# Two passes of the first expert at 208 columns instead of 256

## The chip, the cores and the metric

The kernel runs on one core of a Trainium2 chip. The metric is device time in microseconds of one launch, lower is better. TensorE multiplies, VectorE and ScalarE move and convert, GpSimd (POOL in the profile) issues the transfers with computed addresses, SyncE (SP) most of the others.

## What is computed

A recurrent attention (4 batches, 8 heads, 768 steps, 48 features a head) makes 3072 rows of 384 features; a mixture of 8 experts then works on these rows. Each row goes to the one expert with the largest logit.

```python
for t in range(S):
    cur = np.einsum('bhd,bhe->bhde', u[None] * kt, vt)
    y[:, :, t] = np.einsum('bhd,bhde->bhe', rt, state + cur)
    state = w[None, :, :, None] * state + np.einsum('bhd,bhe->bhde', kt, vt)
...
logits = x @ w_gate
expert_idx = np.argmax(logits, axis=1)
...                                   # rows are numbered within their expert
h = np.maximum(np.einsum('ecd,edf->ecf', disp, w1), 0.0)     # 384 -> 1024
y = np.einsum('ecf,efd->ecd', h, w2)                         # 1024 -> 384
out[i] = gate_w[i] * y[expert_idx[i], pos[i]]
```

With the reference's inputs the first expert gets 380 rows in all, 272 of them from the first 2048 rows; no expert gets more than 410.

## The kernel before, in words

**Attention** works on 24 tiles of 128 steps, one after the other. Behind each tile come its logits and its routing (`route`): the row's number within its expert is counted, and the row is scattered into a buffer in device memory, `xsd`, that has a region for each expert.

**Experts** work in passes. `PASSES` (line 25) has one entry per pass: the expert, the first row, the rows per gathered tile q, the rows of each tile that are handed out qo, and the number of tiles m. A pass fetches m tiles with q rows each from `xsd` (`gather`, line 274), turns them on TensorE to columns (`xtrans`, line 291), so that a pass works on n = m x q columns, and runs two layers. Experts 1 to 7 have one pass of 4 x 104 = 416 columns. The first expert has two: its first rows are taken while the attention still runs (`early_places`, `gather(0)` at tile 20), so that its first pass can start when the attention ends; the second pass does the rest. The first pass gathers tiles of 128 rows of which 80 are handed out, 160 rows in 256 columns; the second has 2 x 128 = 256 rows.

**A product in two parts.** Weights and rows are each split in a high part, in the four-byte type `float32r`, and a rest. A product is three matmuls: high x high, high x rest, rest x high. Layer 1 (`layer1`, lines 308 to 310) makes 8 blocks of 128 outputs from 3 parts of the input, 72 matmuls a pass; layer 2 (`layer2`, lines 327 to 329) makes 3 blocks from 8 parts, 72 as well. Each matmul has its own 128x128 weights. ScalarE makes the high part (`xh` line 295, `hh` line 313), VectorE the rest (`xl` line 296, `hl` line 314), and VectorE copies layer 2's result (`yt`, line 330). `finish` (line 343) turns a tile of the result back and `emit` scales it (line 334) and scatters it to the output (line 335).

**Weights** of the next expert are fetched by SyncE during a pass (line 241) and split by ScalarE and VectorE (lines 249, 250); each `next(ws)` does a piece of it.

**Order.** It is written out by hand: the calls stand in program order, and each engine works in that order. In the last attention tile the first pass's transposes come before the attention's last products; three blocks of its layer 1 are woven into the routing of the last tile. Lines 411 and 92 also matter below: products in full precision (type `float32`), 4 calls of 128 columns, and one of 16 columns a tile.

**When the shortcut fails.** `flags` (line 206) sets a flag if the first 16 tiles (`SNAP`) hold fewer rows of the first expert than `EARLY` while more come later; a branch at the end then does that expert again.

Of the kernel before, what the change touches and what calls it, by code (L numbers as in the profile page):

```python
# [17 lines left out]
NT, DM, E, F = 3072, 384, 8, 1024  # L18
# [2 lines left out]
NI = B * NC  # L21
NP = H // 2
W1S, WL = 416, 416
EARLY, SNAP = 160, 16
PASSES = [(0, 0, 128, EARLY // 2, 2), (0, EARLY, 128, 128, 2)] + [(e, 0, WL // 4, WL // 4, 4) for e in range(1, E)]
XW = 400
FAR = 65536.0
PLAN = [((0, 1, 2), ())] + [((n // 2 + 3,) if n % 2 == 0 and n < 8 else (), (n,)) for n in range(14)]
# [6 lines left out]
def rwkv_moe(nc, tc, dmj, rkv, bdc, wv, wu, uv, wg, w1, w2, out, cap):  # L35
# [4 lines left out]
    with ExitStack() as ctx:  # L40
# [12 lines left out]
        idf = const.tile([128, NI], F32, name="idf")  # L53
        pos = const.tile([128, len(PASSES), 4], F32, name="pos")
        pen = const.tile([128, len(PASSES), 4], F32, name="pen")
        pidx = const.tile([128, len(PASSES), 4], I32, name="pidx")
        cs = const.tile([128, E + 2], F32, name="cs")
# [158 lines left out]
        with ExitStack() as mc:  # L216
# [54 lines left out]
            def gather(k):  # L271
                q, m = PASSES[k][2], PASSES[k][4]
                for i in range(m):
                    nc.gpsimd.indirect_dma_start(out=xg[k % 2][:q, i].bitcast(I32), out_offset=None, in_=xsd[:, :],  # L274
                                                 in_offset=bass.IndirectOffsetOnAxis(ap=pidx[:q, k, i:i + 1], axis=0),
                                                 bounds_check=E * NT - 1, oob_is_err=False)

            def take(k):
                q, m = PASSES[k][2], PASSES[k][4]
                t = keep.tile([128, 4], I32, tag="ids", name=f"ids{k}", bufs=2)  # L280
                g = keep.tile([128, 4], F32, tag="gw", name=f"gw{k}", bufs=2)
                nc.vector.scalar_tensor_tensor(out=t[:q, :m], in0=pen[:q, k, :m], scalar=FAR, in1=xg[k % 2][:q, :m, DM], op0=ALU.mult, op1=ALU.add)
                nc.vector.tensor_copy(out=g[:q, :m], in_=xg[k % 2][:q, :m, DM + 1])
                ids[k] = t, g

            def xtrans(k, j):
                q, m = PASSES[k][2], PASSES[k][4]
                pool, tag, bufs = ((ps1, "a1", 1) if k else (psA, "a0", 2), (ps1, "u", 1), (psA, "a0", 2) if k < 2 else (ps1, "a1", 1))[j]
                tp = pool.tile([128, m * q], F32, tag=tag, name=f"tp{k}_{j}", bufs=bufs)
                for i in range(m):  # L290
                    nc.tensor.transpose(out=tp[:, q * i:q * i + q], in_=xg[k % 2][:q, i, 128 * j:128 * j + 128],  # L291
                                        identity=idn[:q, :q])

                def split():
                    nc.scalar.copy(out=xh[:, j, :m * q], in_=tp)  # L295
                    nc.vector.tensor_tensor(out=xl[:, j, :m * q], in0=tp, in1=xh[:, j, :m * q].bitcast(F32), op=ALU.subtract)  # L296

                return split
# [694 lines left out]
```

## Time and profile before

| | us |
|---|---|
| runs | 396.44, 397.38, 399.80 |
| median | 397.38 |
| the profiled execution | 397.02 |
| its span | 395.3 |

| engine | busy us | share of the span |
|---|---|---|
| TensorE (PE) | 375.1 | 95% |
| weight loads (PEld, beside PE) | 338.4 | 86% |
| VectorE (DVE) | 237.2 | 60% |
| ScalarE (ACT) | 204.4 | 52% |
| GpSimd (POOL) | 137.7 | 35% |

Busy times come from one execution, recorded by the hardware profiler; an engine that waits is not busy. Matmuls overlap, so the distance between the starts of two says more than the duration of one. The attention lies in about the first 136 us, the passes behind it.

### The profile page before, as it was taken

What the parts mean: (1) busy time and instruction counts of PE and PEld (TensorE: products, weight loads), DVE (VectorE), ACT (ScalarE), POOL (GpSimd) and SP (SyncE); (2) the same over time, 40 slices, a digit from 0 to 9 for tenths busy, and PEclk for the clock granted to TensorE, in tenths of its full rate; (3) what the DMA queues carried; (4) which work ended last, traced back from release to release, by engine and by line L of the source; (5) the groups of instructions that cost most, each with busy time, mean ns of one, the idle gap of its engine ahead of it and who ended that gap; (6) DMA issues with size and microseconds to landing.
All of it is one profiled execution on the core that took longest, in us unless ns stands there. A gap on an engine that the chain in (4) does not pass through costs nothing.

```text
span 395.3 us, 9463 instructions
## 1 busy us (share of the span) xinstructions
PE 375.1 (95%) x3587; PEld 338.4 (86%) x3590; DVE 237.2 (60%) x574; ACT 204.4 (52%) x556; POOL 137.7 (35%) x199
## 2 busy tenths in 40 slices
PE   7999999999989789799999999999999999999993
PEld 3677778777767589799999999999999999999992
DVE  6897889898887466554645645645645645643210
ACT  3668787888578334534624624624624624722301
POOL 6122538585673426601501601601601601201203
PEclk9999999999999899999999999999999999999998
DMA  8999878888722546641634644644644644400102
GB/s 174 260 241 263 219 218 236 259 238 264 200 82 71 175 132 189 203 124 21 209 109 131 177 129 133 176 133 133 183 131 127 185 135 129 144 4 16 44 1 70
DMA packets 20633, 59.93 MB, mean 152 GB/s; under 512 B 4303, under 2 KB 4451, under 8 KB 20577
## 3 DMA queue, kind: packets, MB, share of 16 engines
q1 hardware_dynamic: 14848, 44.12, 40.6%
q0 software_dynamic: 5600, 14.72, 11.5%
q8 instruction: 30, 0.49, 0.6%
q10 hardware_dynamic: 128, 0.39, 0.4%
q14 instruction: 27, 0.21, 0.2%
HBM read 49.98 MB, written 10.03 MB: 152 GB/s over the span
## 4 chain that ended last, share of the span: by engine, by line
PE 74%; issue 12%; ACT 5%; DVE 3%; POOL 2%; DMA 1%; POOLq 1%; another core or an unknown queue 0%; SPq 0%; ACTq 0%; DVEq 0%
PE a L310 8%; PE a L309 8%; PE a L308 8%; PE b L327 7%; PE b L328 7%; PE b L329 7%; PE y L565 6%; PE a L522 6%; PE y L556 3%; PE xp L104 3%; PE c L92 2%; ACT s L503 2%; PE c L82 2%; PE tp L291 2%; PE u L534 2%
## 5 line engine op out<-in xcount | busy, mean ns | idle before, releaser
L335 POOL DMA_INDIRECT out<-yo,ids x32 | 32.3, 1009 | 168.1 <-ACT yo L334 166.2
L308 PE MATMUL a<-xh,ws 128*128 128x416 f32 (+1 forms) x216 | 75.3, 349 | 2.2 <-issue 2.0
L313 ACT ACTIVATE hh<-a 128x416 fp32r<-128x416 f32 (+1 forms) x72 | 35.2, 489 | 74.1 <-PE a L310 69.2
L327 PE MATMUL b<-hh,ws 128*128 128x416 f32 (+2 forms) x216 | 73.4, 340 | 0.0
L309 PE MATMUL a<-xl,ws 128*128 128x416 f32 (+1 forms) x216 | 72.5, 336 | 0.1
L310 PE MATMUL a<-xh,ws 128*128 128x416 f32 (+1 forms) x216 | 72.4, 335 | 0.0
L328 PE MATMUL b<-hl,ws 128*128 128x416 f32 (+2 forms) x216 | 71.7, 332 | 0.3 <-issue 0.3
L329 PE MATMUL b<-hh,ws 128*128 128x416 f32 (+2 forms) x216 | 71.5, 331 | 0.0
L314 DVE SCALAR_TENSOR_TENSOR hl<-a,hh 128x416 fp32r<-128x416 f32 (+1 forms) x72 | 39.8, 553 | 50.8 <-ACT hh L313 38.7
L250 DVE TENSOR_TENSOR ws<-wr,ws 128x384 fp32r<-128x384 f32 (+1 forms) x112 | 67.6, 618 | 2.3 <-ACT ws L249 2.3
L503 ACT ACTIVATE s<-eye,l 128x128 f32<-128x128 f32 x168 | 53.8, 392 | 17.2 <-DVE l L93 16.2
L249 ACT CAST ws<-wr 128x384 fp32r<-128x384 f32 (+1 forms) x112 | 60.0, 558 | 2.2 <-DMA xsd<-xr,slot 2.2
L330 DVE COPY yt<-b 128x416 f32<-128x416 f32 (+2 forms) x27 | 14.6, 542 | 66.7 <-PE b L329 64.3
L492 POOL TENSOR_TENSOR P<-dm 112x512 f32<-112x512 f32 x21 | 27.5, 1312 | 48.7 <-DVE dm L508 20.2
L308 PEld LDWEIGHTS a<-xh,ws 128*128 128x128 f32 x216 | 40.7, 188 | 3.3 <-issue 2.4
L328 PEld LDWEIGHTS b<-hl,ws 128*128 128x128 f32 x216 | 40.8, 189 | 0.8 <-issue 0.5
L309 PEld LDWEIGHTS a<-xl,ws 128*128 128x128 f32 x216 | 40.7, 188 | 0.8 <-DVE xl L296 0.5
L329 PEld LDWEIGHTS b<-hh,ws 128*128 128x128 f32 x216 | 40.6, 188 | 0.4
L327 PEld LDWEIGHTS b<-hh,ws 128*128 128x128 f32 x216 | 40.8, 189 | 0.2
L310 PEld LDWEIGHTS a<-xh,ws 128*128 128x128 f32 x216 | 40.6, 188 | 0.4
L274 POOL DMA_INDIRECT xg<-xsd,pidx x32 | 35.0, 1093 | 15.1 <-issue 7.0
L295 ACT CAST xh<-tp 128x416 fp32r<-128x416 f32 (+1 forms) x27 | 12.6, 480 | 52.3 <-PE tp L291 52.3
(147 smaller groups left out, 569.8 us busy)
## 6 DMA issues: line engine op xcount, KB each, us to landing
wr<-w SPq DMA_DIRECT2D x24, 512.0 KB
wr<-w SPq DMA_DIRECT2D x32, 384.0 KB
bd<-bdc SPq DMA_DIRECT2D x24, 384.0 KB
dm<-dmj SPq DMA_DIRECT2D x40, 192.0 KB
dm<-dmj SPq DMA_DIRECT2D x6, 256.0 KB
xg<-xsd,pidx POOLq DMA_INDIRECT x32
out<-yo,ids POOLq DMA_INDIRECT x32
dm<-dmj ACTq DMA_DIRECT2D x2, 192.0 KB
```

The source lines that it names most:

```text
L249: nc.scalar.copy(out=hi, in_=r)
L250: low.append(lambda: nc.vector.tensor_tensor(out=lo, in0=r, in1=hi.bitcast(F32), op=ALU.subtract))
L274: nc.gpsimd.indirect_dma_start(out=xg[k % 2][:q, i].bitcast(I32), out_offset=None, in_=xsd[:, :], in_offset=bass.IndirectOffsetOnAxis(ap=p ...
L308: nc.tensor.matmul(a, lhsT=wh, rhs=xh[:, d, :n], start=d == 0, stop=False)
L309: nc.tensor.matmul(a, lhsT=wh, rhs=xl[:, d, :n], start=False, stop=False)
L310: nc.tensor.matmul(a, lhsT=wl, rhs=xh[:, d, :n], start=False, stop=d == 2)
L313: nc.scalar.activation(hh[:, f, :n], a, AF.Relu)
L314: nc.vector.scalar_tensor_tensor(out=hl[:, f, :n], in0=a, scalar=0.0, in1=hh[:, f, :n].bitcast(F32), op0=ALU.max, op1=ALU.subtract)
L327: nc.tensor.matmul(o, lhsT=wh, rhs=hh[:, f, :n], start=f == 0, stop=False)
L328: nc.tensor.matmul(o, lhsT=wh, rhs=hl[:, f, :n], start=False, stop=False)
L329: nc.tensor.matmul(o, lhsT=wl, rhs=hh[:, f, :n], start=False, stop=f == 7)
L503: nc.scalar.mul(out=s[:, h, p], in_=eye, mul=bon)
```

## The change

`EARLY` goes from 160 to 208. The first pass gathers two tiles of 104 rows and hands out all of them; the second starts at row 208 and has two tiles of 104 rows. Both passes work on 208 columns instead of 256, and together they still cover 416 rows. The condition on the first 16 tiles now asks for 208 rows.

```diff
-EARLY, SNAP = 160, 16
-PASSES = [(0, 0, 128, EARLY // 2, 2), (0, EARLY, 128, 128, 2)] + [(e, 0, WL // 4, WL // 4, 4) for e in range(1, E)]
+EARLY, SNAP = 208, 16
+PASSES = [(0, 0, EARLY // 2, EARLY // 2, 2), (0, EARLY, 104, 104, 2)] + [(e, 0, WL // 4, WL // 4, 4) for e in range(1, E)]
```

On TensorE the two programs have the same 2277 rows in the same order. This is a piece of the difference at the start of the second pass; `tp` is a turned tile, `yp` a turned result, and the sizes are rows by columns of what is written or streamed (the numbers behind names are buffers).

```order
-L291 MATMUL tp_2_2821<-idn,xg_102 128x128 x2
-L343 MATMUL yp_0_2826<-idn,yt 80x128 x3
-L343 MATMUL yp_1_2835<-idn,yt 80x128 x3
-L308 MATMUL a_0_2844<-xh,ws_0_977 128x256
+L291 MATMUL tp_2_2821<-idn,xg_102 128x104 x2
+L343 MATMUL yp_0_2826<-idn,yt 104x128 x3
+L343 MATMUL yp_1_2835<-idn,yt 104x128 x3
+L308 MATMUL a_0_2844<-xh,ws_0_977 128x208
```

No row has changed its place; the turned tile and the matmul of layer 1 have fewer columns, the turned result of the first pass more rows. ScalarE shows the same, here at the end of the attention, where the first pass's tiles are converted (`xh`) between the attention's results (`xs`).

```order
-L295 CAST xh<-tp_0_2418 128x256
-L295 CAST xh<-tp_1_2421 128x256
+L295 CAST xh<-tp_0_2418 128x208
+L295 CAST xh<-tp_1_2421 128x208
 L569 COPY xs_2450<-y_0_2432 128x2x128
 L569 COPY xs_2450<-y_1_2433 128x2x128
```

The two casts stand where they stood, ahead of the copies of the attention's last result, with 48 columns less.

## Rows read from the trace of the kernel before

**Rows 1.** The page's first part: busy us (share of span) xinstructions

```profile
PE 375.1 (95%) x3587; PEld 338.4 (86%) x3590; DVE 237.2 (60%) x574; ACT 204.4 (52%) x556; POOL 137.7 (35%) x199
```

**Rows 2.** Busy us by stage: stretch, length, engines (instructions), PEclk, DMA share, GB/s

```profile
136.00:143.10 7.10, 5.49 (x51) 4.55 (x49) 3.55 (x18) 3.35 (x14) 2.57 (x4) 1.00 0.17 60
143.10:157.70 14.60, 14.29 (x120) 14.05 (x120) 9.68 (x35) 5.49 (x13) 7.75 (x7) 1.00 0.70 205
...
160.00:170.60 10.60, 8.38 (x68) 7.96 (x68) 5.50 (x12) 5.21 (x15) 6.06 (x6) 1.00 0.59 186
170.60:180.30 9.70, 9.70 (x87) 9.70 (x86) 3.92 (x11) 1.99 (x5) 0.00 (x0) 1.00 0.32 97
180.30:383.00 202.70, 202.70 (x1159) 198.56 (x1158) 99.59 (x191) 88.02 (x184) 47.98 (x46) 1.00 0.40 119
```

**Rows 3.** Waits of 128 to 182 us: us in total, times, longest

```profile
PE a L308 <- issue: 2.0, 1, 2.0
...
PEld a L309 <- DVE xl L296: 0.5, 2, 0.3
PE ct L180 <- ACT hh L313: 0.4, 1, 0.4
...
PE b L328 <- issue: 0.3, 1, 0.3
...
PE a L308 <- DVE hl L314: 0.2, 1, 0.2
```

**Rows 4.** Groups by line and shape, whole span: busy us, mean ns, idle before

```profile
L308 PE MATMUL a<-xh,ws 128*128 128x256 f32 x48 | 14.2, 296 | 2.2 <-issue 2.0 <-DVE hl L314 0.2
...
L296 DVE TENSOR_TENSOR xl<-tp,xh 128x416 fp32r<-128x416 f32 x21 | 12.2, 583 | 1.0 <-ACT xh L295 1.0
L291 PE MATMUL tp<-idn,xg 104*128 104x104 f32 x84 | 10.9, 252 | 0.0
L295 ACT CAST xh<-tp 128x416 fp32r<-128x416 f32 x21 | 10.7, 509 | 45.9 <-PE tp L291 45.9
...
L92 PE MATMUL c<-pick,ct 128*128 128x16 f32 x54 | 10.6, 271 | 5.0 <-ACT ct L87 4.3 <-issue 0.4
...
L296 DVE TENSOR_TENSOR xl<-tp,xh 128x256 fp32r<-128x256 f32 x6 | 2.3, 418 | 1.4 <-ACT xh L295 1.4
...
L295 ACT CAST xh<-tp 128x256 fp32r<-128x256 f32 x6 | 2.0, 380 | 6.4 <-PE tp L291 6.4
```

**Rows 5.** Timeline of TensorE: start us, us, line, operation, out<-in, shape, count

```profile
152.03 0.28 PE L327 MATMUL b<-hh,ws 128*128 128x256 f32 x1
...
157.62 0.28 PE L329 MATMUL b<-hh,ws 128*128 128x256 f32 x1
157.74 0.82 PE L291 MATMUL tp<-idn,xg 128*128 128x128 f32 x6
158.39 0.82 PE L343 MATMUL yp<-idn,yt 128*80 128x128 f32 x6
...
159.36 0.39 PE L309 MATMUL a<-xl,ws 128*128 128x256 f32 x1
...
186.17 0.35 PE L309 MATMUL a<-xl,ws 128*128 128x416 f32 x1
...
194.23 0.35 PE L310 MATMUL a<-xh,ws 128*128 128x416 f32 x1
```

**Rows 6.** Timeline of weight loads, 9.9 to 11.2 us

```profile
9.91 0.30 PEld L92 LDWEIGHTS c<-pick,ct 128*128 128x128 f32 x2 [0.65 <-ACT ct L87]
10.13 0.97 PEld L411 LDWEIGHTS gp<-wd,ft 128*128 128x128 f32 x8
11.02 0.21 PEld L458 LDWEIGHTS <-wz 128*128 128x128 bf16 x2
```

**Rows 7.** Timeline of TensorE, transposes of 104 columns

```profile
170.61 0.52 PE L291 MATMUL tp<-idn,xg 104*128 104x104 f32 x4
```

**Rows 8.** Timeline of ScalarE and TensorE around 167 us

```profile
167.03 0.38 ACT L313 ACTIVATE hh<-a 128x256 fp32r<-128x256 f32 x1 [2.76 <-PE a L310]
...
167.93 0.39 PE L308 MATMUL a<-xh,ws 128*128 128x256 f32 x1 [2.04 <-issue]
```

## The prediction

> **What bounds the kernel now.** I read the page first, for the engine that is full; then busy time by stage, to see where the two passes that change lie and whether that engine is still full there; then the waits of that stretch; then the starts of single matmuls and weight loads, because the change alters the size of a matmul and nothing else.
>
> TensorE is busy 95% of the span, no other engine over 60% [rows 1]. By stage [rows 2] the two passes of the first expert run from about 136 to 180.3 us. TensorE is full in 143.1 to 157.7 (14.29 of 14.60 us) and in 170.6 to 180.3 (9.70 of 9.70). It has holes in 136 to 143.1 (5.49 of 7.10), where the routing of the last tile is woven in, and in 160 to 170.6 (8.38 of 10.60). From 180.3 to 383 it is busy all 202.70 us. So what these two passes win or lose on TensorE goes straight to the end: behind them nothing waits that could swallow it. The granted clock is 1.00 in all these stages, the 2.4 GHz level.
>
> The holes in the passes' own work [rows 3] are one wait of 2.0 us before L308, one of 0.3 before L328, and small ones of 0.2 to 0.5 us behind evictions.
>
> **The change, part by part.** No row is moved, added or removed on TensorE: shapes change, and nothing else. Five things get a price.
>
> *The 288 matmuls, 256 columns before, 208 after* (72 in each layer of each pass; [rows 4] has L308's 48, and the other five lines have as many). What counts is not the duration of one (296 ns there, they overlap) but the distance between starts. From 152.03 to 157.62 us stand 48 matmuls of 256 columns: 5.59 / 47 = 0.119 us each. From 186.17 to 194.23 stand 44 of 416: 8.06 / 43 = 0.187 [rows 5]. That is 0.068 us for 160 columns, 0.43 ns a column. Were columns all that counts, 208 would take 0.119 - 48 x 0.00043 = 0.098 us.
>
> But each of these matmuls has a weight load of its own, 128x128 of four-byte data, whatever its columns. How fast such loads can follow one another is seen where the matmul is short: L411's eight loads start at 10.13 and the next line's at 11.02, so they are 0.89 / 8 = 0.111 us apart, with 128 columns per matmul; as the eight are shown to last 0.97 us, one lasts 0.97 - 7 x 0.111 = 0.19, and L92's two, 0.30 us together, start 0.30 - 0.19 = 0.11 us apart, with 16 columns per matmul [rows 4, 6]. From 128 columns down to 16 nothing is won, so this is the load. At 256 columns the interval (0.119) stands just above that floor, at 208 the columns alone (0.098) would lie under it. I take the floor, 0.111: L411's row is the nearest in columns. The saving is 0.119 - 0.111 = 7.6 ns before rounding. I count 261 matmuls: the 27 of the first three blocks of layer 1 lie in the stage from 136 to 143.1, where TensorE waits for others. 261 x 7.6 ns = **2.0 us**. Bounds: 0 (the interval stays), and 261 x 20.6 ns = 5.4 us (columns alone).
>
> The Trainium skill, "TensorE: Matmul & The Clock Gate", section "Back-to-back issue gap", gives columns / 2.4 + 2.5 ns for a lone matmul: an estimate of 89 ns at 208, 20 ns under its 109 at 256, which by itself would give 5.2 us. Its section "LDWEIGHTS (loading the stationary operand)" gives columns of the weights / 1.2, 107 ns for 128, which sets against that a floor close to the 0.11 us of the rows; no run so far shows which of the two binds at 208.
>
> *The 12 transposes* (L291), 128 columns before, 104 after. Six start at 157.74 and the next line at 158.39: 0.108 us each; four of 104 columns take 0.52 us, one of them 0.25: (0.52 - 0.25) / 3 = 0.09 each [rows 4, 5, 7]. Six lie on the full path: **0.1 us**. The other six lie in 131 to 136, ahead of waits: nothing.
>
> *Evictions* with 48 columns less. ScalarE's cast takes 380 ns at 256 and 509 at 416, 0.81 ns a column, 39 ns saved; VectorE's subtraction 418 and 583, 1.03 a column, 49 ns saved [rows 4]. They are hidden behind TensorE except at the small waits (twice for xl, once for hh, once for hl) [rows 3]: about 0.09 each where both stand in the chain, **0.3 us**, or nothing if another releaser is next.
>
> *Outputs.* The first expert's four result tiles have 104 rows where they had 80, 80, 128, 128. ScalarE's multiply there keeps its 384 columns. The gathers fetch 104 rows for 128, the scatters as many tiles as before. All this lies behind full stretches of TensorE: nothing.
>
> *The count the early pass relies on.* The first pass now wants 208 rows of the first expert among the first 16 tiles, where it wanted 160. From the reference's inputs there are 272, and the expert has 380 in all, under 416. The branch that would do the expert again is not taken: nothing.
>
> Sum, against the profiled execution's own 397.02 us (its span of 395.3 and 1.7 around it): 397.02 - 2.0 - 0.1 - 0.3 = **394.6 us**. The median of the three runs is 397.38, 0.4 above that execution; one per cent either side of it is 393.4 and 401.4, about what a measurement of this kernel can tell from no change.
>
> **The rivals.**
> *Columns alone count* (the load hides better than I think). For it: at 256 and 416 the interval follows the columns. Against: L92 and L411 stop at 0.11. It gives 397.02 - 5.4 - 0.4 = 391.2 us. The skill's gap formula above points this way.
>
> *The gain is lost to a wait that TensorE does not set.* At 167.03 ScalarE starts L313, 2.76 us after its last work, although the last matmul of the block it reads, the fourth block of nine, was started by 159.36 + 34 x 0.119 = 163.4; TensorE's L308 follows at 167.93 [rows 5, 8]. The trace names no reason for ScalarE's late start. If its moment is fixed by something else, all that is won before 167.93 is lost, and only the 90 matmuls behind it count: 90 x 7.6 ns = 0.7, 396.2 us with 0.1 for the rest. The 0.3 us before L328 [rows 3] could grow in the same way. Against: if ScalarE is late by its place in its own program, the delay moves along with the work. If the late start goes away altogether, up to 2.0 us are won on top.
>
> *Slower: narrow four-byte matmuls lose their rate.* This is the one that ends on the other side. The matmuls with operands in the rounded four-byte type run at 0.43 ns a column, about one period of 2.4 GHz, and every row of that kind in the trace has 256 columns or more. All four-byte work with fewer goes at about two periods a column or slower: transposes of 128 columns 0.108 us, of 104 columns 0.09 [rows 4, 5, 7], and L411, a product in full precision, takes two instructions of 0.111 us for each of its four calls [rows 6]. Should 208 columns fall under that rule, one costs 208 x 0.85 = 177 ns, and 288 x 58 ns = 16.8 us: 414 us. If each also had to be done twice, like L411, 354 ns and 288 x 235 = 67.7 us: 465 us. The point that decides is whether the fast rate hangs on the number of columns, somewhere between 208 and 256. Against it: the built instruction streams of TensorE have the same length in both kernels, and in those 288 matmuls the column count is all that differs, so no slower form is chosen when the program is made; only the engine itself could do so. No row of the trace contradicts it, so it keeps a chance that is not small.
>
> **How the numbers follow.** Load-bound at about 0.111 us: 0.60, at 394.6, with 393.0 to 396.0 around it (a floor of 0.107 to 0.115). Columns alone: 0.12, at 391.2. Gain lost in a wait: 0.13, at 396 to 398. Narrow matmuls slow: 0.15, at 414 to 465. The likeliest is 394.6. The range that leaves out the slow rival and little else is 391.0 to 398.0; the likeliest one's own is 393.0 to 396.0. Faster by over 1% (under 393.4): the 0.12 and a small part of the first case, 0.17. Slower by over 1%: 0.15, and 0.01 for what I don't see: 0.16. Within 1%: 0.67.
>
> **What would show it right or wrong.** In the profile after, 48 matmuls of layer 2 in the first pass that took 5.59 us should take 47 x 0.111 = 5.2 us; 4.6 us would speak for columns alone, 5.6 for no effect, 8.3 or more for the slow rival. The weight loads should start 0.111 us apart, each right behind the one before. ScalarE's row that is now late by 2.76 us should be about as late, and shifted to the left with the rest. The stretch of pass 2 to the end should last the same, from its first L308 on (now 180.28), and start 2.4 us sooner. The prediction is wrong if the interval is anything but 0.107 to 0.115 us, or if a hole grows by more than a microsecond.

## The result, and the profile after

The changed kernel took 392.78 us in the median of four runs (391.35 to 394.80), the kernel before 397.40 beside it; the ratio is 0.989, 95% interval 0.985 to 0.994. Two later comparisons on other chips, with more runs, gave 0.993 (0.990 to 0.996) and 0.993 (0.989 to 0.997). In microseconds that is 4.3 the first time and 2.8 both other times, where 2.4 were forecast (the medians themselves lie 4.6, 3.4 and 3.7 us apart). 392.78 lies inside the range given (391.0 to 398.0) and just under the likeliest case's own (393.0 to 396.0); against the bound of 1% it came out faster by 1.1% once and within the bound, by 0.7%, twice. The kernel's own time differs between chips: the kernel before took 387.9, 394.9, 395.0 and 397.6 us on four of them. So times are compared on one chip only.

The page of the profile after (span 391.0 us, 395.3 before), its busy times, as in [rows 1]:

```profile
PE 373.2 (95%) x3587; PEld 337.6 (86%) x3590; DVE 236.5 (60%) x574; ACT 203.7 (52%) x556; POOL 138.8 (36%) x199
```

Busy time by stage, columns as in [rows 2] (the last three numbers are the granted clock, the DMA share and GB/s):

```profile
131.00:136.00 5.00, 5.00 (x50) 3.99 (x48) 3.38 (x18) 2.02 (x7) 1.42 (x2) 0.66 0.45 149
136.00:143.10 7.10, 5.51 (x49) 4.94 (x49) 4.34 (x26) 2.66 (x10) 1.76 (x3) 0.92 0.29 87
143.10:157.70 14.60, 14.60 (x125) 14.60 (x123) 9.31 (x32) 5.89 (x16) 8.01 (x7) 0.92 0.66 196
...
160.00:170.60 10.60, 10.17 (x91) 9.81 (x89) 7.39 (x18) 5.15 (x15) 5.53 (x5) 1.00 0.83 243
170.60:180.30 9.70, 9.70 (x76) 9.61 (x75) 3.20 (x7) 2.62 (x6) 0.00 (x0) 1.00 0.08 33
180.30:383.00 202.70, 202.70 (x1163) 198.38 (x1162) 98.43 (x189) 87.71 (x184) 49.73 (x48) 1.00 0.41 119
```

Two things differ from before that no step of the forecast had: TensorE has no hole of 2 us in 160 to 170.6 (10.17 busy, 8.38 before), and the granted clock is 0.92, not 1.00, in the two stages around 143 us: for some 3 us it stood at 1.2 GHz. In 131 to 136 us the kernel before has the same 0.66.

Waits of TensorE in 128 to 182 us, as in [rows 3]:

```profile
PE rk L145 <- DVE oh L138: 1.1, 1, 1.1
PE c L92 <- ACT ct L87: 1.0, 1, 1.0
...
PE a L308 <- DVE hl L314: 0.4, 2, 0.3
```

Groups by line and shape, as in [rows 4]:

```profile
L308 PE MATMUL a<-xh,ws 128*128 128x208 f32 x48 | 14.7, 305 | 0.4 <-DVE hl L314 0.4
...
L296 DVE TENSOR_TENSOR xl<-tp,xh 128x208 fp32r<-128x208 f32 x6 | 2.0, 369 | 1.3 <-ACT xh L295 1.3
L295 ACT CAST xh<-tp 128x208 fp32r<-128x208 f32 x6 | 1.7, 340 | 6.7 <-PE tp L291 6.7
```

TensorE's timeline: the 48 matmuls of layer 2 in the first pass that answer to the first of [rows 5], the first two and the last of them, and the six transposes behind them:

```profile
151.12 0.27 PE L327 MATMUL b<-hh,ws 128*128 128x208 f32 x1
151.23 0.28 PE L328 MATMUL b<-hl,ws 128*128 128x208 f32 x1
...
156.37 0.28 PE L329 MATMUL b<-hh,ws 128*128 128x208 f32 x1
156.48 0.70 PE L291 MATMUL tp<-idn,xg 104*128 104x104 f32 x6
157.02 0.82 PE L343 MATMUL yp<-idn,yt 128*104 128x128 f32 x6
```

(156.37 - 151.12) / 47 = 0.112 us from start to start, where it was 0.119. The duration of one matmul (305 ns for L308, 296 before) did not show this: they overlap.

From the starts of the first L308 of each pass, the lengths of the passes can be read in every profile. This table carries the rest of the text; "hole" is what TensorE waits before L308 in the second pass, "clock" says whether a stretch at the lower level (1.2 GHz) lies in the first pass.

| profile | columns | first pass starts | first pass, us | second pass, us | clock | hole, us |
|---|---|---|---|---|---|---|
| before | 256, 256 | 135.94 | 23.03 | 21.31 | full | 2.0, 0.2 |
| changed | 208, 208 | 134.76 | 22.83 | 18.51 | lower | 0.4 |
| before again | 256, 256 | 134.24 | 24.13 | 19.07 | lower | 0.2 |
| e1_pad_256 | 256, 256 | 134.29 | 24.11 | 19.83 | lower | 0.9 |
| e2_second_208 | 256, 208 | 133.76 | 23.16 | 19.14 | full | 0.9 |
| e3_first_160 | 160, 256 | 133.94 | 22.20 | 21.33 | full | 1.2, 0.9 |
| a1_after_again | 208, 208 | 132.76 | 23.05 | 17.68 | lower | none |
| a2_after_third | 208, 208 | 134.56 | 22.59 | 19.92 | full | 0.8, 1.0 |
| e4_gathers_later | 256, 256 | 133.65 | 23.24 | 18.56 | full | none |
| e6_filled_wait | 208, 208 | 133.82 | 22.49 | 19.04 | full | 0.9 |
| e7_both | 208, 208 | 133.67 | 22.47 | 17.65 | full | none |
| e7_again | 208, 208 | 128.31 | 22.38 | 17.57 | full | none |
| e9_splits_later | 208, 208 | 128.43 | 20.92 | 18.17 | full | none |
| e10_fetch_later | 256, 256 | 128.56 | 24.11 | 18.57 | lower | none |

From the third pass to the end of TensorE's work all profiles have 208.2 to 208.4 us.

### The profile page after: what moved, and what is told of

It reads as the page before. It is cut to its first block, busy times and chain, and to the rows that moved or that the text cites. A ratio compares the mean times of both kernels' runs of the same rounds, so it can differ in the third digit from the quotient of the medians.

```text
span 391.0 us, 9463 instructions
## 1 busy us (share of the span) xinstructions
PE 373.2 (95%) x3587; PEld 337.6 (86%) x3590; DVE 236.5 (60%) x574; ACT 203.7 (52%) x556; POOL 138.8 (36%) x199
## 4 chain that ended last, share of the span: by engine, by line
PE 73%; issue 12%; ACT 7%; DVE 3%; POOL 2%; DMA 1%; POOLq 1%; SPq 0%; ACTq 0%; DVEq 0%
PE a L310 8%; PE a L309 8%; PE a L308 8%; PE b L327 7%; PE b L329 7%; PE b L328 7%; PE y L565 5%; PE a L522 5%; PE y L556 3%; ACT s L503 3%; PE xp L104 3%; PE c L92 2%; POOL out L335 2%; PE yp L343 2%; PE tp L291 2%
## 5 line engine op out<-in xcount | busy, mean ns | idle before, releaser
L308 PE MATMUL a<-xh,ws 128*128 128x416 f32 (+1 forms) x216 | 75.8, 351 | 0.4 <-DVE hl L314 0.4
L313 ACT ACTIVATE hh<-a 128x416 fp32r<-128x416 f32 (+1 forms) x72 | 34.5, 480 | 74.3 <-PE a L310 70.3
L310 PE MATMUL a<-xh,ws 128*128 128x416 f32 (+1 forms) x216 | 72.8, 337 | 0.0
L328 PE MATMUL b<-hl,ws 128*128 128x416 f32 (+2 forms) x216 | 71.1, 329 | 0.0
L314 DVE SCALAR_TENSOR_TENSOR hl<-a,hh 128x416 fp32r<-128x416 f32 (+1 forms) x72 | 39.1, 543 | 50.6 <-ACT hh L313 42.9
L249 ACT CAST ws<-wr 128x384 fp32r<-128x384 f32 (+1 forms) x112 | 60.0, 557 | 0.6 <-DVE hl L314 0.6
L308 PEld LDWEIGHTS a<-xh,ws 128*128 128x128 f32 x216 | 41.7, 193 | 1.3 <-DVE hl L314 0.8
L309 PEld LDWEIGHTS a<-xl,ws 128*128 128x128 f32 x216 | 41.6, 193 | 0.7 <-DVE xl L296 0.5
L310 PEld LDWEIGHTS a<-xh,ws 128*128 128x128 f32 x216 | 41.6, 192 | 0.4
L274 POOL DMA_INDIRECT xg<-xsd,pidx x32 | 35.8, 1118 | 15.1 <-issue 7.0
L328 PEld LDWEIGHTS b<-hl,ws 128*128 128x128 f32 x216 | 40.9, 189 | 0.2
```

The lines of the kernel that those rows point to most:

```text
L249: nc.scalar.copy(out=hi, in_=r)
L308: nc.tensor.matmul(a, lhsT=wh, rhs=xh[:, d, :n], start=d == 0, stop=False)
L309: nc.tensor.matmul(a, lhsT=wh, rhs=xl[:, d, :n], start=False, stop=False)
L310: nc.tensor.matmul(a, lhsT=wl, rhs=xh[:, d, :n], start=False, stop=d == 2)
L314: nc.vector.scalar_tensor_tensor(out=hl[:, f, :n], in0=a, scalar=0.0, in1=hh[:, f, :n].bitcast(F32), op0=ALU.max, op1=ALU.subtract)
L328: nc.tensor.matmul(o, lhsT=wh, rhs=hl[:, f, :n], start=False, stop=False)
```

## The experiments

### Is it the columns, and is there a floor?

**e1_pad_256.** The rows are split as in the change, the columns padded back.

```diff
-PASSES = [(0, 0, EARLY // 2, EARLY // 2, 2), (0, EARLY, 104, 104, 2)] + ...
+PASSES = [(0, 0, 128, EARLY // 2, 2), (0, EARLY, 128, 104, 2)] + ...
```

> The change with both passes padded to 256 columns again (tiles of 128 rows, 104 of them handed out; EARLY stays 208): the split of the rows is that of the change, the columns are those of before. Theory (interval set by the weight load at 208 columns): the distance between matmul starts goes back from 112 to 119 ns, 1.0 us a pass; so about 392.8 + 2.0 = 394.8 us if no wait comes with it, and 396.8 if the 2.0 us hole of TensorE in front of L308 in the second pass comes back as well. Rival (the gain comes from the split of the rows, not from the columns): 392.8 us. Theory of the hole (TensorE's done signals reach ScalarE late while GpSimd issues the four gathers L274): the program has the timing of before again around these gathers, so the hole should be there, 1 to 2 us, between 162 and 170 us; a rival by which the hole was a chance event of the one execution makes it absent.

Measured: 394.79 us, ratio to the kernel before 0.999 (0.995 to 1.002). The interval is 0.119 us again. The split of the rows alone is worth nothing that can be measured, nor does the profile show a gain: the first pass takes 24.11 us, and 24.13 in the second profile of the kernel before, both with the lower clock in it. So it is the columns. The hole is there, with 0.9 us.

**e2_second_208.** Only the second pass narrowed.

```diff
-PASSES = [(0, 0, EARLY // 2, EARLY // 2, 2), (0, EARLY, 104, 104, 2)] + ...
+PASSES = [(0, 0, 128, EARLY // 2, 2), (0, EARLY, 104, 104, 2)] + ...
```

> EARLY 208; the first pass padded to 256 columns, only the second pass at 208. Theory (interval): first pass 119 ns between starts, second 112; the second pass gains 1.0 us by its matmuls, so 1.0 us over the changed kernel at most, 393.8 us, and less if the half-clock stretch of the changed kernel at 142 to 145 us stays away (it cost it about 1.1 us in the first pass): then 392.7. Theory of the hole: whether it is there depends on which matmul block ends while GpSimd issues the gathers L274 of the second pass; the late signals themselves (a start of ScalarE's L313 more than 0.5 us behind the end of its block) are there in any case, the hole is 0 to 2 us. Rival (narrow matmuls of the second pass themselves remove the hole): no late signal at all.

Measured: 394.90 us, ratio 0.999 (0.996 to 1.003); 0.119 us in the first pass, 0.112 in the second. The hole of 0.9 us stands in a pass of 208 columns, so narrow matmuls do not remove it. The ratio alone can't tell 0.9 us from nothing.

**e3_first_160.** The kernel before with an even narrower first pass.

```diff
-PASSES = [(0, 0, 128, EARLY // 2, 2), (0, EARLY, 128, 128, 2)] + ...
+PASSES = [(0, 0, EARLY // 2, EARLY // 2, 2), (0, EARLY, 128, 128, 2)] + ...
```

> The kernel before with its first pass at 2 tiles of 80 rows, 160 columns, instead of 2 x 128; the second pass stays at 256 columns. Theory (a floor set by the weight load): 0.111 us between matmul starts, as at 208 columns, the 48 matmuls of layer 2 of the first pass take 5.2 us; the time is that of before less 0 to 1.1 us (0 if a half-clock stretch takes it back): 396.3 to 397.4. Rival (columns set the interval, and 208 columns lie on it by chance): 160 x 0.43 ns + the constant part of 8 ns, about 0.078 us, 3.7 us for the 48; 2.9 us less for the pass, 394.5. Rival (few columns lose the fast rate): 160 x 0.85 = 136 ns or more, 6.5 us for the 48, and 399 us or more.

Its four runs took 393.9, 394.2, 404.2 and 404.5 us, too far apart for a ratio; it is read by its profile, that of the run of 394.2 us. The same 48 matmuls of layer 2, first, second and last:

```profile
149.49 0.28 PE L327 MATMUL b<-hh,ws 128*128 128x160 f32 x1
149.60 0.27 PE L328 MATMUL b<-hl,ws 128*128 128x160 f32 x1
...
154.74 0.27 PE L329 MATMUL b<-hh,ws 128*128 128x160 f32 x1
```

5.25 us with 160 columns, 5.25 with 208: the interval is 0.112 us in both. It is a floor that the number of columns does not move. Columns alone (3.7 us) and a slow rate for few columns (6.5) are both out.

Whether the weight load sets this floor, as the prediction argues, no run tests: each of these matmuls has one load, and loads and matmuls start equally far apart. It is not a floor for every matmul that has a load of its own. The kernel before has these rows of bf16 products, with as many loads as matmuls:

```profile
99.84 0.19 PE L147 MATMUL rk<-oh,ones 128*128 128x16 bf16 x2
122.27 0.17 PE L147 MATMUL rk<-oh,ones 128*128 128x8 bf16 x1
L147 PEld LDWEIGHTS <-ones 128*128 128x128 bf16 x15 | 0.9, 97 | 0.1
```

Two of them start about 0.02 us apart, and four-byte transposes whose loads have 104 rows instead of 128 start 0.09 us apart [rows 7]. That fits a floor set by a load of 128x128 four-byte values, and does not prove it.

### The hole in front of L308

**e8_before_again.** The kernel before, unchanged, profiled once more.

> The kernel before once more, unchanged, for a second profile of it. Theory (the hole in front of L308 comes from the order of the program, with GpSimd's gathers L274 running beside the second pass's layer 1): there again, 2.0 us within 0.3, at the same matmul block, and ScalarE's L313 late again at the same place. Rival (a chance event of the one profiled execution): no hole, or one of another size or at another place, and a profiled time of about 395. The end of the attention: if the 1.2 us by which the first pass of the changed kernel starts sooner (134.76 against 135.94) are variation between executions, this profile's start of that pass may lie anywhere within some 1.5 us of 135.9; if the change made it, it lies at 135.9.

Measured: 394.38 us, span 392.6. Busy time by stage, and TensorE's waits before L308 in 128 to 182 us:

```profile
143.10:157.70 14.60, 14.60 (x114) 14.60 (x114) 9.07 (x29) 5.40 (x13) 7.95 (x7) 0.90 0.60 187
160.00:170.60 10.60, 10.44 (x88) 10.21 (x88) 7.56 (x18) 6.18 (x16) 5.74 (x6) 1.00 0.75 228
```

```profile
PE a L308 <- ACT xh L295: 0.2, 1, 0.2
PE a L308 <- DVE hl L314: 0.2, 1, 0.2
```

No hole, a first pass that starts 1.7 us sooner, and a lower clock in a stage where the first profile had 1.00. So three things that set the two first profiles apart, the hole, the end of the attention and the clock, differ about as much between two profiles of one and the same program. This one is from a chip on which the kernel before took 395.0 us, not 397.4, but hole and clock differ on that one chip too: e1_pad_256 has a hole of 0.9 us with as many columns, and the first pass of e2_second_208, the same as that of e1_pad_256, keeps the full clock. It takes no change of the program to make these differences.

**a1_after_again, a2_after_third.** The changed kernel, unchanged, twice more.

> The changed kernel once more, timed in more rounds, because the kernel before was seen to vary: in its second profile TensorE had no hole in front of L308 and the first pass started 1.7 us sooner. Theory (the change itself is worth the shorter matmul interval, 2 x 72 x 7 ns = 2.0 us, and 0.3 for transposes and evictions, and the rest of the first comparison's 4.6 us was the difference between executions): 2.3 us below the kernel before on this chip, about 392.7 where that one takes 395.0. Rival (the change also takes the hole away for good): 4.6 us below, 390.4. Rival (the freed time goes into other waits): 0 to 1 us below.

> The changed kernel once more, for its ratio on one more chip. In the last runs the kernel before took 387.9 us where it had taken 394.9 and 395.0, and no signal of TensorE came more than 0.3 us late, in the attention too: the late signals belong to the chip or its state. Theory: where they are absent (the kernel before at about 388), the change is worth its columns alone, 2.0 + 0.3 us or a ratio of 0.994, less up to 1.1 where a half-clock stretch falls into the first pass; where they are present (the kernel before at about 395), what it gains or loses at the holes in front of L308 comes on top, 0.988 to 0.996. Rival (the columns' gain is swallowed by ScalarE's wait in front of L249 in the first pass, which the run with the splits moved showed, and only the second pass gains): 0.9 us, 0.9975, where the late signals are absent.

Measured: 391.45 beside 394.86 (ratio 0.993), and 393.90 beside 397.62 (0.993). The first has no hole; in the second it is back, in the changed kernel. Its timeline, TensorE and ScalarE, idle time and its end in brackets:

```profile
164.62 0.36 PE L308 MATMUL a<-xh,ws 128*128 128x208 f32 x1 [0.82 <-issue]
166.83 0.36 PE L308 MATMUL a<-xh,ws 128*128 128x208 f32 x1 [0.95 <-DVE hl L314]
```

```profile
161.63 0.35 ACT L313 ACTIVATE hh<-a 128x208 fp32r<-128x208 f32 x1 [1.01 <-PE a L310]
163.82 0.34 ACT L313 ACTIVATE hh<-a 128x208 fp32r<-128x208 f32 x1 [1.44 <-PE a L310]
166.03 0.34 ACT L313 ACTIVATE hh<-a 128x208 fp32r<-128x208 f32 x1 [1.46 <-PE a L310]
```

ScalarE stands idle and starts late; [rows 8] show the same. The last expectation's rival (only the second pass gains) is neither shown nor excluded by the ratio.

**e4_gathers_later.** What is late is the signal that a block is done: the profile ends ScalarE's waits with a signal of L310, and at 163.82 and 166.03 us the matmul that it tells of had been over for 2.0 and 3.2 us. The kernel before, with the four gathers of the third expert's rows, which GpSimd issues here, taken out of this stretch:

```diff
-                if 1 < k < len(PASSES) - 1:
+                if 2 < k < len(PASSES) - 1:
                     gather(k + 1)
...
                         finish(k - 1, f - 1)
+                    if k == 2 and f == 1:
+                        gather(3)
```

> The kernel before (256 columns in both passes) with the four gathers L274 of the third expert's rows issued after the first result tile of the second pass, in the pass behind it, so that GpSimd issues no gather while the second pass runs its layer 1. Theory (TensorE's done signals come late while GpSimd issues these gathers): ScalarE's L313 of the second pass starts within 0.1 us of the end of its block wherever it waits for one, no start 0.5 us late or more, and no hole of TensorE in front of L308; since four profiles of programs with 256 columns in a pass had holes of 2.0, 0.9, 0.9 and none there, 0 to 2 us are won, about 1.0: 394.0 where the kernel before takes 395.0. Rival (the late starts have another cause, the output scatters L335 or the weight fetches): late starts and holes as before, 395.0. Rival (the gathers delay the signals wherever they run): late starts during the next pass's layer 1, whose blocks are longer (1.7 us), so holes there of 0 to 1 us, 394.5.

Measured: 393.44 beside 394.86, ratio 0.995 (0.993 to 0.998): 1.4 us less in the medians, 1.9 by the ratio. The timelines of ScalarE and of the last matmuls of the blocks; blocks 4 to 6 of the second pass:

```profile
161.71 0.39 ACT L313 ACTIVATE hh<-a 128x256 fp32r<-128x256 f32 x1 [0.22 <-PE a L310]
162.78 0.39 ACT L313 ACTIVATE hh<-a 128x256 fp32r<-128x256 f32 x1 [0.28 <-PE a L310]
163.85 0.39 ACT L313 ACTIVATE hh<-a 128x256 fp32r<-128x256 f32 x1 [0.28 <-PE a L310]
```

```profile
161.40 0.28 PE L310 MATMUL a<-xh,ws 128*128 128x256 f32 x1
162.46 0.28 PE L310 MATMUL a<-xh,ws 128*128 128x256 f32 x1
163.53 0.28 PE L310 MATMUL a<-xh,ws 128*128 128x256 f32 x1
```

These three L313 start 0.31 or 0.32 us behind the start of their block's last matmul, that is 0.03 behind its end; none of the eight starts more than 0.1 behind it. In the kernel before, with the gathers beside it, this is so up to the second block, and then the distance grows. The fourth block's last matmul, and the gathers on GpSimd:

```profile
163.47 0.28 PE L310 MATMUL a<-xh,ws 128*128 128x256 f32 x1
```

```profile
162.36 1.10 POOL L274 DMA_INDIRECT xg<-xsd,pidx  x1 [0.31 <-issue]
163.76 1.09 POOL L274 DMA_INDIRECT xg<-xsd,pidx  x1 [0.30 <-PE a L310]
165.15 1.06 POOL L274 DMA_INDIRECT xg<-xsd,pidx  x1 [0.30 <-issue]
166.52 1.07 POOL L274 DMA_INDIRECT xg<-xsd,pidx  x1 [0.30 <-issue]
```

163.47 to ScalarE's 167.03 [rows 8] is 3.56 us, 3.25 more than on time. With the gathers gone from the stretch the late starts are gone, all eight, and 1.4 to 1.9 us with them. That is shown for this place. The same holds for e7_both below, which has the gathers moved too. In each of the nine profiles that have the gathers here, the chip of e10_fetch_later aside, some L313 starts 1.9 to 3.7 us behind the end of its block, also where TensorE has no hole. So the lateness comes every time, and how much of it reaches TensorE varies. In e8_before_again, without a hole, the sixth block's last matmul and its L313:

```profile
165.02 0.28 PE L310 MATMUL a<-xh,ws 128*128 128x256 f32 x1
167.20 0.38 ACT L313 ACTIVATE hh<-a 128x256 fp32r<-128x256 f32 x1 [0.72 <-PE a L310]
```

In e4_gathers_later the gathers run from 182 us on, beside blocks of 1.7 us; there ScalarE starts on time (a block that ends at 184.68, L313 at 184.72), so gathers do not delay the signal wherever they run.

**e10_fetch_later.** The gathers left in place, the weight fetches beside them held back.

```diff
                     if e < E:
+                        if k == 1:
+                            nc.sync.dma_start(out=scr, in_=hh[:, 7, 0:8].bitcast(F32))
                         ws = wstream(e, PLAN)
```

> The kernel before (256 columns, gathers L274 where they were), with the weight fetches L241 of the third expert held back on SyncE until the second pass's layer 1 is through (a small transfer that waits for its last block stands ahead of them in SyncE's queue), so that the gathers run without 1.5 MB of weights beside them. Late signals were seen with gathers and fetches together (162 to 168 us), none with the fetches alone (the run with the gathers moved). Theory A (the gathers alone do it): ScalarE's L313 still starts 0.5 us or more behind the end of its block during the gathers, and TensorE's hole is 0 to 2 us as before. Theory B (gathers and fetches together do it): every L313 starts within 0.1 us of the end of its block, no hole, 393.5 where the kernel before takes 394.9 or so, unless the later fetches are missed by the third pass.

Measured: 388.41 beside 387.85, ratio 1.001 (1.000 to 1.002). All eight L313 are on time. But this chip showed no late signal anywhere, in the attention neither (the latest there is 0.1 us behind its matmul's end; in every profile of the other chips it is more than 0.5 us, up to 1.3), and the kernel before took 7 us less on it. So the run decides nothing between gathers alone and gathers with fetches.

### The wait in front of the routing

**e6_filled_wait** and **e7_both.** The fourth block of layer 1 moved ahead of the product L145, for which TensorE waits 1.1 us; e7_both has the later gathers too.

```diff
             third = layer1(0, 2)
+            fourth = layer1(0, 3)
             advance()
...
-            layer1(0, 3)()
+            fourth()
```

> The changed kernel with only the fourth block of layer 1 of the first pass put ahead of the routing product L145. Theory: the wait of 1.1 us before L145 shrinks to about 0.1, 1.0 us less than the changed kernel, 391.7 where the kernel before takes 395.0; the matmuls behind it run at the full granted clock, as TensorE no longer pauses there. Rival (half-clock stretches come and go with the execution, as the profiles at 256 columns had one in two of four): as many of them as without the fill, and the 1.0 us alone.

> The changed kernel with the gathers L274 moved as in the run above, and with the fourth block of layer 1 of the first pass (nine matmuls of 0.112 us, 1.0 us) put ahead of the routing product L145 that TensorE waits 1.1 us for. Theory: 2.3 us from the columns, about 1.0 from the gathers, 1.0 from the filled wait: 390.7 where the kernel before takes 395.0; and 1.1 less where the half-clock stretch that the profile of the changed kernel has at 142 to 145 us followed from the wait. Rival (the routing, the gather of the second pass and so its start become later by as much): 391.7 or more.

Measured: 392.44 (ratio 0.994, 0.990 to 0.998), not below the changed kernel's 391.45; and 390.57 (0.989, 0.984 to 0.993). The wait before L145 is gone, but the first pass is 22.5 us long, only 0.1 under the 22.59 of a2_after_third. So 390.57 meets the 390.7 that were expected, but the 1.0 us for the filled wait is not in it. Where the gain went, in the timelines of ScalarE and TensorE of e7_both:

```profile
142.12 0.34 ACT L313 ACTIVATE hh<-a 128x208 fp32r<-128x208 f32 x1 [0.78 <-PE a L310]
145.80 0.62 ACT L249 CAST ws<-wr 128x512 fp32r<-128x512 f32 x1 [3.34 <-DMA xsd<-xr,slot]
146.32 0.34 ACT L313 ACTIVATE hh<-a 128x208 fp32r<-128x208 f32 x1
...
148.37 0.36 PE L328 MATMUL b<-hl,ws 128*128 128x208 f32 x1 [0.30 <-DVE hl L314]
149.25 0.36 PE L328 MATMUL b<-hl,ws 128*128 128x208 f32 x1 [0.30 <-DVE hl L314]
```

ScalarE stands 3.34 us in front of the second expert's first weight split, which waits for the scatter of the last attention tile to land, with L313 of the sixth to the eighth block queued behind it. TensorE reaches layer 2 sooner and waits there instead, 0.3 us twice before L328.

**e9_splits_later, e7_again.** e7_both with these splits behind the four blocks, beside e7_both on one chip.

```diff
             for f in range(4, 8):
                 layer1(0, f)()
-                next(ws)
+            next(ws)
             flags(sm)
             for d in range(3):
                 layer2(0, d)
                 next(ws)
+                next(ws)
```

> The run with both moves (gathers later, fourth block ahead of the routing), and besides the second expert's first weight splits (ScalarE's L249 with VectorE's L250) issued behind the last four blocks of the first pass instead of between them. In the profile of the run before it ScalarE stands 3.3 us in front of L249, waiting for the scatter of the last attention tile to land (the weights go into memory that the tile held), with L313 of the blocks 5 to 7 queued behind it, and TensorE then pauses at L328 three times, about 1.1 us in all. Theory (that queue returns what the filled wait had won): L313 of these blocks runs ahead of L249, the pauses at 147 to 149.3 us go, the first pass takes 22.5 - 1.0 = 21.4 us instead of 22.5, and the time is 1.0 us below the run with both moves. Rival (the splits, started later, are late for something else, the products of the third pass or VectorE's copies L330): no gain, or a new wait at the end of the first pass or in front of the third.

> The run with both moves (gathers later, fourth block ahead of the routing) once more, for the comparison on one chip with the run that also moves the weight splits: 390.6 where the kernel before takes 394.9, 1.0 above that run by the theory told there, and level with it by the rival.

Measured: 384.48 and 385.67 beside 387.85, ratios 0.992 (0.990 to 0.993) and 0.995 (0.993 to 0.996). ScalarE and TensorE of e9_splits_later:

```profile
139.39 0.34 ACT L313 ACTIVATE hh<-a 128x208 fp32r<-128x208 f32 x1 [1.16 <-PE a L310]
140.39 0.34 ACT L313 ACTIVATE hh<-a 128x208 fp32r<-128x208 f32 x1 [0.66 <-PE a L310]
140.76 3.64 ACT L249 CAST ws<-wr 128x512 fp32r<-128x512 f32 x7
...
150.36 0.36 PE L309 MATMUL a<-xl,ws 128*128 128x208 f32 x1 [0.67 <-DVE xl L296]
```

L313 of all blocks now runs ahead of these splits, and the first pass falls from 22.38 to 20.92 us. Part of it returns: the second pass starts with a wait of 0.67 us for VectorE, which has the splits' other half in front of `xl`, and takes 18.17 instead of 17.57. 1.2 us remain in the medians, 0.9 in the two spans (382.5 and 383.4). This version is 3.3 us under the kernel before, on a chip that had no late signals to save. The changed kernel was not run there; that this version beats it too is likely, and not shown: its passes take 20.92 + 18.17 = 39.1 us, where the three profiles of the changed kernel have 40.7 to 42.5, each with a hole or the lower clock in it.

## Why the prediction was right, and where it was not

**The floor: right in size.** 0.111 us was forecast for the interval, 0.112 measured, and 5.25 us for the 48 matmuls (5.2 forecast). It held at 160 columns too. Its cause, the weight load, stays argued (e3_first_160). One of the rows behind it carried less than the prediction thought: L411's 0.111 us for 128 columns could as well be the columns, at the pace of the transposes (0.108 us for 128), as the slow rival reads it; it was L92, with 16 columns, that spoke for a floor. The Trainium skill, "TensorE: Matmul & The Clock Gate", section "LDWEIGHTS (loading the stationary operand)", gives the columns of the weights / 1.2: an estimate of 107 ns for this floor, 5 under the trace. The formula for a lone matmul in its section "Back-to-back issue gap" gives an estimate of 89 ns at 208 columns, which the trace does not have; the section itself says that in a stream of loads and matmuls both set the distance.

**The sum: its mechanism was right, the terms were a little large.** In the second pass the profiles without holes give 18.56 and 18.57 us at 256 columns, and 17.68, 17.65 and 17.57 at 208: 0.9 us, where 1.1 for the matmuls and 0.1 for the transposes stood in the sum. In the first pass, at full clock, 23.03 to 23.24 became 22.59: 0.4 to 0.7 us, where 117 matmuls were to bring 0.9. The reason, by the rows, is ScalarE's wait in front of L249, seen in e7_both: the matmuls get shorter, the scatter's landing does not move. ScalarE's sixth L313 starts 12.67 us behind the start of the pass in a2_after_third and 12.68 to 12.93 in the three profiles at 256 columns; only behind it is the rest shorter, 9.9 us for 10.2 to 10.4. TensorE's wait before L328 was 0.5 us in a2_after_third, 0.3 in [rows 3]. The rival on lost gains had named this place. Where the first pass runs partly at the lower clock, that wait is covered: 24.1 became 22.83 and 23.05, 1.1 to 1.3 us. So the columns are worth 1.3 to 2.2 us by the profiles. The repeated ratios say 2.8, with intervals of 1.7 to 4.0 and 1.3 to 4.4 us; what may lie between is not settled.

**The first comparison's 4.3 us of span: one step failed.** The step "ScalarE's row that is now late by 2.76 us should be about as late" took what one execution showed for a property of the program. That ScalarE is late is one, on most chips; by how much, and what of it reaches TensorE, is not. TensorE waited 2.2 us before L308 in the second pass of the profile of before, and 0.4 in that of after; the first pass started 1.2 us sooner. Against that, the lower clock in the first pass of after cost 0.9 to 1.1 us there (24.1 against 23.0 to 23.2 at 256 columns). 1.0 from the second pass's columns, 1.8 from the hole, 1.2 from the end of the attention, and 0.2 from the first pass, its gain less the clock: 4.2 of the 4.3. So 3.0 of it came from differences that profiles of one and the same program show among each other, and about 1 was lost to another of that kind. Where 392.78 us lies in the range is in good part chance. The rival had the clause that up to 2.0 us are won if the late start goes away, but not why it should.

**The slow rival: out.** No matmul of 160 or 208 columns lost its rate.

**The transposes: as priced.** Six took 157.02 - 156.48 = 0.54 us, where they had taken 0.65 [rows 5]: 0.1 us.

**Evictions: as priced, and hidden.** The cast fell from 380 to 340 ns, the subtraction from 418 to 369, 40 and 49 ns as forecast; the small waits behind them vary more from profile to profile than that.

**The third pass to the end:** 208.25 us, 208.28 before; nothing swallows what the two passes win.

## What to carry to other kernels

Where every matmul has weights of its own, measure the interval between starts at two or three widths before narrowing: below the width where a floor takes over (here between 208 and 256 columns), columns cost nothing and save nothing. Take a second profile of the kernel before, before a hole of one execution goes into a sum; where a releaser was long done, the size of the hole can be chance. When a wait is filled, look at which engine stands in front of a transfer next and what is queued behind it, and move that with it.

## What was not expected of the hardware

**TensorE's signal that a block is done can reach ScalarE microseconds late.** It was on time without the gathers and up to 3.25 us late with them, at the same place. It also depends on the chip, or on the state that it was in. The run with both moves, on two chips, busy time in 60 to 128 us of the attention, first e7_both, then e7_again:

```profile
60.00:128.00 68.00, 64.84 (x1121) 51.08 (x1120) 57.32 (x148) 51.54 (x174) 45.78 (x49) 1.00 0.64 194
```

```profile
60.00:128.00 68.00, 66.13 (x1189) 53.01 (x1186) 61.63 (x172) 53.95 (x182) 47.11 (x51) 1.00 0.68 206
```

TensorE gets 1.3 us more done in that stretch on the second chip, and the first pass starts 5.4 us sooner in the same program. Why gathers delay the signal at 162 us and not at 182, and why not on that chip, stays open.

**The clock.** Five of ten profiles with the 1.1 us wait in front of L145 have a stretch of some 3 us at 1.2 GHz in the first pass, none of the four in which the wait is filled. In the stage where it fell, TensorE was busy 5.51 of 7.10 us in the profile after, and 5.49 in that of before, which kept the full clock. That the filled wait keeps the clock up is possible, and not shown: if the wait had no part in it, four profiles drawn from these fourteen would still all be free of such a stretch about one time in eight.
